# A two-layer kernel whose body is written as per-batch lists of single operations

## The chip, the cores and the metric

One core of one Trainium2 chip. The metric is the device time of one execution in microseconds (us); TensorE's granted clock is given where it bears on a reading. TensorE is called PE, VectorE DVE, ScalarE ACT, GpSimd POOL and SyncE SP, as in the profile.

## The reference

Attention with a threshold, then a gated layer that mixes over the sequence. Batch 8, 8 heads, 576 positions, head size 64; in and out are float32.

```python
scores = q @ k.T / 8                              # per batch and head: 576 x 576
scores = where(scores >= max(scores) - tau, scores, -1e9)
attn   = softmax(scores)
x      = concat_heads(attn @ v)                   # 8 x 576 x 512

h = relu(x @ w_in); u, v = h[..., :512], h[..., 512:]
v_s = w_spatial @ normalize(v) + b_spatial        # mixes positions
out = (u * v_s) @ w_out
```

## The kernel before

The work is cut into 144 steps, 18 for each batch. A step makes the scores of 128 queries of two heads in a three-bank PSUM tile, of which there are two. TensorE writes the main part (512 keys) in four 64x64 quadrants and the tail (the last 64 keys of both heads) with one 128x128 product. VectorE takes the maximum, ScalarE the exponential in two halves, then the mask makes p: on VectorE as one instruction, or, for some steps, on ScalarE (a steep Prelu in place of the first exponential, an exponential after it, and a small shift of the maximum on VectorE). p is transposed by a DMA and multiplied with v ("pv"). The gated layer's jobs (v, u, s, o) of earlier batches are spread over the steps.

```python
def on_act(i, c):                       # which masks ScalarE makes
    return c in (2, 4) or c == 0 and 0 < i < 6

def scores(i, c):
    s = ps_s.tile([P, 1536], F32, name="s")       # pool of two
    ...                                           # 4 main products, 64x64 quadrants
    for n, m, rows in tails:                      # the tail, straight behind them
        nc.tensor.matmul(out=view(s[rows], 512, ...), lhsT=qks[n][:, 0, m],
                         rhs=kd_ring[n % 2], start=True, stop=True)

def step(i, c, fs):                     # fs: this step's other jobs (multiply, evict)
    s = scores(i, c)
    while held: held.pop(0)()           # evictions left by the step before
    for kind, mm, ev in fs[:2]:
        mm()
        if kind == "act": ev()
    nc.vector.tensor_reduce(out=nm, in_=s, ..., op=ALU.max, negate=True)
    ...                                 # shift, VectorE evictions, exponentials
    if unmasked: mask()                 # mask and transpose of the step before
    for f in ready: f()                 # loads, stores, transposes of x
    for kind, mm, ev in fs[2:]:
        mm(); ...

# x: one transpose for each head pair (4 blocks of 128x128) and one per two pairs for their ends
nc.sync.dma_start_transpose(out=xts[b][:, hp, 0:512]..., in_=xn...)
nc.sync.dma_start_transpose(out=xts[b][:, hp, 512:640], in_=xn)

# ahead of the body: q, k, v of the first pairs, then
for j in range(3):
    load_w_in(j)
```

## Time and profile before

| | before |
|---|---|
| median of 4 runs (range) | 480.91 us (479.03 to 484.21) |
| span of the profiled run | 480.6 us, clock 0.992 |
| busy PE / DVE / ACT / POOL | 443.8 / 411.7 / 390.6 / 227.3 us |
| SP's time in issuing DMAs, summed from the trace | 381.5 us |

A batch is cut where its first maximum starts. The lines behind this are in the prediction.

### The profile page before, as it was taken

To read this page: it belongs to the slowest core of one execution; us is meant where nothing else is said; L and a number is where in the kernel's file an instruction comes from. 1 tells how busy PE (TensorE), PEld (TensorE's weight loads), DVE (VectorE), ACT (ScalarE), POOL (GpSimd) and SP (SyncE) were. 2 spreads that over 40 slices of the span, in tenths; PEclk is the share of its full clock that TensorE was granted. 3 is DMA by queue.
4 is the path that set the end of the run, shared out by engine and by line. 5 is a ranking of instruction groups with operands and counts; after the bars stand their busy time and mean duration, and the time that the engine had idled before them with its cause. 6 is when DMAs were issued, how large, how long until landed. Compare 5 with 4: busy or idle time off the path is not lost.

```text
span 480.6 us, 10876 instructions
## 1 busy us (share of the span) xinstructions
PE 443.8 (92%) x4153; PEld 225.9 (47%) x4203; DVE 411.7 (86%) x563; ACT 390.6 (81%) x677; POOL 227.3 (47%) x403
## 2 busy tenths in 40 slices
PE   7788888889999999999999999999997999999995
PEld 4344444444544445454544545444543545445542
DVE  4989898979989988999889997999887898898573
ACT  4799999989878897888889798888977689797251
POOL 3453344995347533674327553575416544253021
PEclk9899999999999999999999999999999999999999
DMA  7989899979999999988999899899999889667523
GB/s 231 247 179 210 191 222 195 206 158 210 196 164 189 195 199 205 236 151 176 221 211 183 160 210 224 178 192 200 194 192 168 180 164 217 136 114 119 149 86 112
DMA packets 226131, 88.55 MB, mean 184 GB/s; under 512 B 196896, under 2 KB 221600, under 8 KB 226080
## 3 DMA queue, kind: packets, MB, share of 16 engines
q1 hardware_dynamic: 225424, 86.98, 87.7%
q8 instruction: 33, 0.54, 0.5%
q0 software_dynamic: 160, 0.52, 0.3%
q10 hardware_dynamic: 496, 0.36, 0.2%
q14 instruction: 18, 0.15, 0.1%
HBM read 33.31 MB, written 9.44 MB: 89 GB/s over the span
## 4 chain that ended last, share of the span: by engine, by line
PE 45%; DVE 22%; ACT 22%; issue 7%; DMA 3%; POOL 0%; POOLq 0%; SPq 0%; ACTq 0%; DVEq 0%
PE s L576 14%; DVE negm L618 10%; DVE p L599 8%; ACT e L635 6%; PE s L580 6%; ACT e L641 5%; PE f L295 4%; PE f L478 4%; PE f L246 3%; ACT p L637 3%; PE f L537 2%; DMA pT<-p 2%; PE f L508 2%; ACT vrel L446 2%; PE f L290 2%
## 5 line engine op out<-in xcount | busy, mean ns | idle before, releaser
L618 DVE TENSOR_REDUCE negm<-s 128x2 f32<-128x1152 f32 x144 | 194.9, 1353 | 32.5 <-PE s L580 31.3
L576 PE MATMUL s<-qkT 64*64 64x512 f32 x1152 | 158.6, 621 | 14.5 <-ACT e L641 8.6
L599 DVE SCALAR_TENSOR_TENSOR p<-e,ctau 128x1152 bf16<-128x1152 f32 x91 | 133.7, 1469 | 1.2 <-ACT e L641 1.2
L641 ACT ACTIVATE e<-s,negm 128x576 f32<-128x576 f32 x182 | 124.9, 741 | 7.2 <-DVE negm L618 6.8
L580 PEld LDWEIGHTS s<-kd,qkT 128*128 128x128 f32 (+1 forms) x320 | 41.6, 178 | 118.4 <-issue 106.3
L635 ACT ACTIVATE e<-s,negm 128x576 f32<-128x576 f32 x106 | 72.9, 742 | 15.8 <-DVE negm L622 10.6
L269 POOL COPY kd<-qkT 64x64 f32<-64x64 f32 x62 | 28.0, 451 | 98.5 <-ACT qkT L264 96.7
L580 PE MATMUL s<-kd,qkT 128*128 128x128 f32 (+1 forms) x320 | 70.1, 323 | 0.0
L576 PEld LDWEIGHTS s<-qkT 64*64 64x64 f32 x1152 | 30.1, 132 | 46.6 <-ACT e L641 18.7
L454 POOL TENSOR_SCALAR nmean<-sm 128x1 f32<-128x1 f32 (+1 forms) x35 | 16.6, 474 | 71.1 <-ACT vrel L446 63.1
L295 PEld LDWEIGHTS <-pT 128*128 128x128 bf16 x1024 | 41.8, 97 | 9.1 <-issue 5.9
L295 PE MATMUL f<-v,pT 128*128 128x65 bf16 x992 | 44.9, 194 | 0.0
L637 ACT ACTIVATE p<-e 128x1152 bf16<-128x1152 f32 x37 | 43.0, 1163 | 1.2
L137 POOL COPY qn<-ql 128x640 f32<-128x640 f32 x31 | 32.6, 1052 | 16.2 <-DMA ql<-in_k_dram 11.6
L290 PE MATMUL f<-v,pT 128*128 128x130 bf16 x124 | 27.2, 219 | 7.0 <-DMA pT<-p 3.5
L508 PE MATMUL f<-wsT,vn 128*128 128x512 bf16 x119 | 31.1, 382 | 0.3
L466 POOL TENSOR_SCALAR vn<-vrel,rs,nm 128x512 bf16<-128x512 f32 (+1 forms) x34 | 28.5, 839 | 3.7
L478 PE MATMUL f<-xT,w_in 128*128 128x512 bf16 x97 | 27.6, 379 | 1.6 <-DVE xn L304 0.8
L436 PE MATMUL f<-w_in,xT 128*128 128x512 bf16 x102 | 28.2, 379 | 0.5
L253 ACT COPY qkT<-f 128x512 f32<-128x512 f32 x31 | 18.3, 590 | 12.8 <-PE f L246 12.2
L251 ACT ACTIVATE qkT<-f 128x512 f32<-128x512 f32 x31 | 18.3, 589 | 12.5 <-PE f L246 12.1
L304 DVE TENSOR_TENSOR xn<-f,r 128x256 bf16<-128x256 f32 x62 | 26.3, 425 | 2.1
(168 smaller groups left out, 647.9 us busy)
## 6 DMA issues: line engine op xcount, KB each, us to landing
vl<-in_v_dram SPq DMA_DIRECT2D x16, 512.0 KB, 4.5
ql<-in_q_dram SPq DMA_DIRECT2D x15, 512.0 KB, 4.9
kl<-in_k_dram SPq DMA_DIRECT2D x15, 512.0 KB, 4.4
out_dram<-oo SPq DMA_DIRECT2D x10, 512.0 KB, 3.6
uT<-in_moe_w_in_dram SPq DMA_DIRECT2D x3, 512.0 KB, 6.1
uT<-in_moe_w_spatial_dram SPq DMA_DIRECT2D x2, 576.0 KB, 5.6
vl<-in_v_dram SPq DMA_DIRECT2D x16, 64.0 KB, 4.3
pT<-p SPq DMA_TRANSPOSE x64, 5.0
```

Of the source, the lines that this page charges most:

```text
L137: nc.gpsimd.tensor_copy(out=t, in_=ld_ring[i // 2 % 2][w][:, 2 * (i % 2):2 * (i % 2) + 2].rearrange("p h c d -> p c h d"))
L290: nc.tensor.matmul(out=t[:, at:at + 130], lhsT=pt[:, 4, :], rhs=vt[:, 4:6, :].rearrange("p b d -> p (b d)"), start=True, stop=False)
L295: nc.tensor.matmul(out=t[:, at + 65 * h:at + 65 * h + 65], lhsT=pt[:, 5 * h + j, :], rhs=vt[:, 6 * h + j, :], start=False, stop=(h == 1 an ...
L478: nc.tensor.matmul(out=t, lhsT=w_in[:, m, f * P:(f + 1) * P], rhs=xts[b][:, m, 0:512], start=(m == 0), stop=(m == 3))
L508: nc.tensor.matmul(out=t, lhsT=vn[:, c, f * P:(f + 1) * P], rhs=wsT[:, c, 0:512], start=(c == 0), stop=(c == 4))
L576: nc.tensor.matmul(out=s[rows, 1024 * h:1024 * h + 512], lhsT=qks[n][halves[h], 0, m], rhs=qks[n][halves[h], 1, 0:512], start=True, stop=True)
L580: nc.tensor.matmul(out=view(s[rows], 512, [[448, 2], [1, 64]]), lhsT=qks[n][:, 0, m], rhs=kd_ring[n % 2], start=True, stop=True)
L599: nc.vector.scalar_tensor_tensor(out=pt[:, c % 2, :], in0=ef, scalar=ctau, in1=ef, op0=ALU.is_ge, op1=ALU.mult)
L618: nc.vector.tensor_reduce(out=nm, in_=s, axis=AX.X, op=ALU.max, negate=True)
L635: nc.scalar.activation(out=e[:, h, :], in_=s[:, h, :], func=ACT.Prelu, bias=nm[:, h:h + 1], scale=by, alpha=1e30)
L637: nc.scalar.activation(out=pr_ring[i // 2 % 2] if c == 4 else p_ring[2 * (i % 2) + c // 2][:, c % 2], in_=e.rearrange("p h s -> p (h s)"), ...
L641: nc.scalar.activation(out=e[:, h, :], in_=s[:, h, :], func=ACT.Exp, bias=nm[:, h:h + 1])
```

## The change

The intent is to let each engine have its own order. The body is no longer generated by `step`; it is a list of tokens for each batch. S is the main scores of a step, K their tail, M the maximum, B the shift, E and F the two exponentials, W a mask on VectorE, Z one on ScalarE, T a transpose of p, X one of x, L a load, Ci a load of w_in, and so on; ":1" means the batch before. There are four lists, the last serving batches 3 to 7. The order of the tokens is the order in which each engine gets its instructions.

```diff
+ORDER = [( ... ),            # 203, 240, 252 and 248 tokens
+ "S0:0 QA1:0 K0:0 qa1:0 v4:2 M0:0 S1:0 ev4:2 W17:1 QR1:0 K1:0 qr1:0 u1:2 E0:0 kd1:0 M1:0 F0:0 R1:1 "
+ ... )]
+ON_ACT = [(2, 4, 5, 9, 11, 13, 16), (0, 2, 4, 11, 13), (2, 4, 11, 13, 16), (2, 4, 7, 11, 13, 15)]
-    def scores(i, c): ...
-    def step(i, c, fs): ...
+    def main_scores(g): ...        # token S
+    def tail_scores(g): ...        # token K
+    def top(g): ...                # token M
+    ...
-                sends.append(lambda: nc.sync.dma_start_transpose(     # x, 4 blocks per head pair
-                    out=xts[b][:, hp, 512:640], in_=xn))              # and 1 for the ends
+    def send_x(m, n0, n1):                                            # two pairs and their ends
+        nc.sync.dma_start_transpose(out=to..., in_=xns[m][:, n0:n1, :]...)
-    ld_ring ... ("ql", 5), ("kl", 4), ("vl", 5)                       # ends loaded per two pairs
+    rest_ring, vx_ring                                                # ends loaded per batch
-        for j in range(3):
-            load_w_in(j)                                              # now tokens Ci2, Ci1, Ci0
+        for it in range(B):
+            for tok in ORDER[min(it, len(ORDER) - 1)].split():
+                run_token(tok, it)
```

## The prediction

> **What bounds the kernel now.** I read the page's engine table first, then busy time cut at every 18th maximum (a batch has 18 steps, each begun by one TENSOR_REDUCE on a score tile), then the costliest groups, the list of waits, and the timeline of one step and of the longest stall.
>
> The engine table: three engines are above 80%, so the average names no bound.
>
> ```profile
> PE 443.8 (92%) x4153; PEld 225.9 (47%) x4203; DVE 411.7 (86%) x563; ACT 390.6 (81%) x677; POOL 227.3 (47%) x403
> ```
>
> Busy time by stretch: the opening, batches 0, 1, 2, 4, 6, and the ending. Columns are the stretch, its length, busy us of each engine with the number of instructions, granted clock, DMA share, GB/s.
>
> ```profile
> 0.00:9.28 9.28, 6.62 (x35) 4.48 (x36) 3.62 (x26) 3.23 (x6) 3.27 (x14) 1.00 0.71 203
> 9.28:55.92 46.64, 38.79 (x367) 19.09 (x365) 41.52 (x51) 40.27 (x60) 21.57 (x39) 0.96 0.90 213
> 55.92:108.35 52.43, 44.42 (x459) 23.73 (x464) 46.33 (x60) 49.26 (x85) 32.14 (x54) 1.00 0.99 196
> 108.35:162.20 53.85, 51.20 (x506) 26.66 (x511) 49.05 (x63) 46.61 (x84) 30.20 (x52) 1.00 0.99 191
> ...
> 217.68:272.56 54.88, 53.60 (x507) 26.96 (x513) 49.65 (x63) 47.55 (x85) 28.18 (x49) 1.00 0.95 194
> ...
> 327.44:387.12 59.68, 55.21 (x507) 27.35 (x513) 49.75 (x63) 47.82 (x85) 27.86 (x49) 0.97 0.95 183
> ...
> 441.50:480.60 39.10, 33.86 (x260) 17.28 (x265) 21.55 (x51) 14.72 (x29) 5.55 (x7) 0.99 0.41 118
> ```
>
> Three regimes. Batch 0 has no second layer: PE is idle 7.9 us, DVE busy 89%, ACT 86%. Batch 1 is ScalarE's: 49.26 of 52.43 (94%). From batch 2 on PE is the bound: 53.60 of 54.88, 98%, with the DMA queues at 95 to 99% beside it. Batches 3, 5 and 7 took 55.48, 54.88 and 54.38. Batch 6 is the odd one, 4.8 us over its neighbours. The groups that I price with:
>
> ```profile
> L618 DVE TENSOR_REDUCE negm<-s 128x2 f32<-128x1152 f32 x144 | 194.9, 1353 | 32.5 <-PE s L580 31.3
> L599 DVE SCALAR_TENSOR_TENSOR p<-e,ctau 128x1152 bf16<-128x1152 f32 x91 | 133.7, 1469 | 1.2 <-ACT e L641 1.2
> L641 ACT ACTIVATE e<-s,negm 128x576 f32<-128x576 f32 x182 | 124.9, 741 | 7.2 <-DVE negm L618 6.8
> L637 ACT ACTIVATE p<-e 128x1152 bf16<-128x1152 f32 x37 | 43.0, 1163 | 1.2
> ```
>
> The timeline of one step in batch 4, then the stall of batch 6:
>
> ```profile
> 252.03 1.09 PE L576 MATMUL s<-qkT 64*64 64x512 f32 x8
> 253.05 0.49 PE L580 MATMUL s<-kd,qkT 128*128 128x128 f32 x2
> 253.38 1.03 PE L436 MATMUL f<-w_in,xT 128*128 128x512 bf16 x4
> ...
> 358.94 6.81 SPq L603 DMA_TRANSPOSE pT<-p  x1
> ...
> 369.36 0.23 PE L290 MATMUL f<-v,pT 128*128 128x130 bf16 x1 [3.19 <-DMA pT<-p]
> ...
> 371.49 1.99 PE L576 MATMUL s<-qkT 64*64 64x512 f32 x8
> ```
>
> Each PE job starts before the modelled end of the last one, so start to start counts: scores 1.02 us, their tail 0.33, four bf16 products 0.86. In batch 6 a transpose of p landed late, PE waited 3.19 us, and its next score set took 1.99 us instead of 1.09.
>
> **What the Trainium skill says.** "Perfetto Trace Analysis", Identifying the Most-Contended Engine, warns that matmul busy share is a poor measure of PE's headroom; here the starts support the 98%, since groups follow each other with no gap. "TensorE: Matmul & The Clock Gate", HAM oscillation, says an idle gap of some 3.4 us lets the clock fall; the trace agrees, with a gap of 3.19 us and a score set at half speed after it, mean clock 0.97. "SBUF — State Buffer", Who interferes with whom, says a VectorE instruction with two SBUF inputs and a GpSimd instruction that reads SBUF exclude each other; the mask is one of those, and a q copy that met it took 1.90 us against 0.72 us alone at 8.09. "DMA: Bandwidth & Descriptors", DMA Transpose (X-bar), says two transposing streams at once corrupt each other, so all of them stay on one queue; in the trace every transpose is issued by SP, and one of p holds that queue about 3.3 us.
>
> **The change part by part.**
> 1. The body. Each of the eight batches is now a written list of single operations, so maximum, shift, two halves of the exponential, mask, product and eviction each have their own place on their engine. Matmul work does not change: the instruction order has 5,261 PE rows against 5,260. No PE time is removed; only waits can be. The last two tokens and the remaining jobs leave the same nine gMLP jobs of batch 6 for after the body, so the ending is worth nothing: 39.1 stays. The opening loads and the first transposes are the same too: 9.3 stays.
> 2. Masks on ScalarE: batch 0 has 7 instead of 9, batch 1 5 instead of 8, batch 2 5 instead of 6, later 6 as before (one step moved). A mask leaving ScalarE saves it 1.16 us and costs VectorE 1.47 less the 0.25 us shift = 1.22. So batch 0: ACT 40.3 - 2.3 = 38.0, DVE 41.5 + 2.4 = 43.9. Batch 1: ACT 49.3 - 3.5 = 45.8, DVE 46.3 + 3.7 = 50.0. Batch 2: DVE 50.3, still under PE's 51.2. The bound of batch 1 changes engine and hardly falls.
> 3. SP queue. x is transposed for two head pairs and their ends in one piece: 38 transposes of x become 15, at 1.2 to 1.3 us of issue each, so about 28 us less. The 64-row ends of q, k, v are loaded per batch: 65 loads become about 34, at 0.62 us about 19 us less. 47 us over eight batches is 6 us of queue per batch, of about 44 used. Bytes fall only by the double load of v's ends, about 0.5 MB of 88.55, so the DMA engines stay as full as they are. This lies off the critical path except where a transpose of p comes late, as in batch 6.
> 4. w_in is loaded in the list instead of ahead of it: 2 MB no longer stand before the second group's q and k. At 13.9 to 19.6 us only POOL waited for these, so I give it nothing.
>
> Sum. A two-buffer cycle (scores 1.35, maximum 1.35, exponentials 1.37, some 0.8 for shift and handovers, an estimate) makes 4.9 us per two steps, 44 us for 18, and VectorE 43.9: batch 0 goes from 46.6 to 45.5. Batch 1: VectorE's 50.0 at 97%, 51.5. Batch 2: 53.2. Batch 3: 54.3. Batches 4 and 5: PE's 53.6 at 99%, 54.2 each. Batch 6: most of its 4.8 us goes with the lighter queue, 55.0. Batch 7: 53.6. With 9.3 and 39.1 that is 9.3 + 45.5 + 51.5 + 53.2 + 54.3 + 108.4 + 55.0 + 53.6 + 39.1 = 469.9, so 470 us, 2.1% less. Of the 10.7 us, 4.7 come from the stall of batch 6, 2.0 from batches 0 and 1, the rest from 0.7 to 1.2 us in each later batch.
>
> **The rivals.**
> Saturation: PE and DMA are both full, and the list only moves waits about. For it: PE's 98% and a DMA share of 0.95 to 0.99. Against it: 33 us of PE idle time in the whole run, a third of it in batches 0 and 1. Then 476 to 480.
> VectorE becomes the bound: it takes six more masks, 7.3 us, in batches where it had 88 to 91%; POOL's exclusions come on top. The list of waits puts 31.3 us of its idle time to score tails, so it can only fill that if scores come earlier. Then batches 0 to 2 keep their length: 473 to 477.
> Rigid order: each engine obeys one fixed order, with two PSUM banks for all jobs and two score tiles; a late operation holds what stands behind it, and a PE gap near 3 us also halves the clock. For it: the stall of batch 6 shows the price, some 5 us. A burst of a store, a merged x transpose and a 512 KB load ahead of a p transpose would repeat in each steady batch. Then 480 to 490.
> Better than expected: PE alternates now between scores and other jobs before the tail. Before, the tail follows the scores at 1.02 us in every step, so no row shows what another neighbour costs; 0.05 us per step would be 7 us either way. With that and no stall, 460 to 464.
>
> **Range and chances.** My sum is just at the 2% line (470.6). The better case and the sum's good side make 50% for faster; saturation and VectorE make 46%; the rigid order mostly ends within 2%, and 4% is left for slower. Range 461 to 480.
>
> **What would show it.** Right: steady batches of 54.0 to 54.5 us with PE at 99%; no PE wait of 3 us on a transpose of p and clock 1.00 in batch 6; batch 1 at 51 to 52 with DVE near 97% and ACT near 88%; SP idle longer; opening and ending within 0.5 us. Wrong: a steady batch under 53 (then PE's busy time held removable cost), or over 55; batch 0 or 1 shorter by over 3 us (then the cycle and not VectorE's work was the limit); new waits of PE for evictions by ScalarE; or an ending that moves by over 2 us.

## The result, and the profile after

| | before | after |
|---|---|---|
| median of 4 runs (range) | 480.91 us (479.03 to 484.21) | 463.68 us (462.81 to 464.75) |
| ratio | | 0.964 (95%: 0.958 to 0.969) |
| opening | 9.3 | 9.5 |
| batch 0, 1, 2 | 46.6, 52.4, 53.9 | 44.5, 51.1, 53.1 |
| batch 3, 4, 5 | 55.5, 54.9, 54.9 | 52.1, 53.4, 53.6 |
| batch 6 | 59.7 | 53.6 |
| batch 7 and ending | 93.5 | 91.3 |

Ratios are the mean time of one kernel's fast runs over that of the other's in the same rounds, so not quite the ratio of the medians. Rows below the ratio are from the two profiled runs.

The engine table of the changed kernel:

```profile
PE 430.0 (93%) x4147; PEld 224.2 (49%) x4203; DVE 417.7 (90%) x558; ACT 380.1 (82%) x673; POOL 209.2 (45%) x434
```

PE has 13.8 us less busy time, with the same matmuls; a few us of this are missing records, since runs of the changed list whose traces lack none have PE busy for 433.3 us (masks elsewhere) to 436.1 (w_in earlier), and the kernel before, profiled again, 443.8. The stretches show where: opening, batches 0, 1, 2, 4, 6, ending, with the columns explained in the prediction.

```profile
0.00:9.45 9.45, 7.46 (x37) 5.10 (x41) 3.72 (x22) 3.26 (x6) 2.06 (x9) 1.00 0.73 207
9.45:53.93 44.48, 37.19 (x368) 18.50 (x361) 42.57 (x50) 37.89 (x59) 16.34 (x34) 1.00 1.06 238
53.93:105.01 51.08, 45.43 (x462) 23.37 (x467) 49.12 (x58) 45.61 (x81) 31.44 (x58) 1.00 0.96 194
105.01:158.12 53.11, 50.70 (x505) 26.64 (x512) 51.47 (x64) 45.17 (x83) 32.51 (x63) 1.00 0.94 190
...
210.18:263.55 53.37, 50.95 (x504) 26.74 (x510) 50.28 (x64) 46.56 (x84) 24.29 (x53) 1.00 0.99 200
...
317.13:370.74 53.61, 51.29 (x506) 26.91 (x512) 50.43 (x64) 46.77 (x85) 24.78 (x53) 1.00 0.98 203
...
420.69:462.01 41.32, 35.87 (x300) 18.63 (x301) 23.35 (x53) 16.32 (x32) 7.42 (x13) 0.99 0.40 114
```

In batch 4 PE is busy 50.95 us where it was 53.60, with 504 matmul records against 507. Both lack some, the changed kernel more. Here are batches 4 and 5 together in two traces that lack none (4203 of 4203): the kernel before, profiled again, and the changed list with w_in loaded earlier (its order differs in batch 0 alone):

```profile
218.16:327.90 109.74, 107.97 (x1027) 53.95 (x1025) 100.04 (x127) 95.05 (x169) 57.15 (x98) 1.00 0.98 196
```

```profile
216.32:322.59 106.27, 103.81 (x1026) 53.56 (x1024) 99.92 (x128) 93.67 (x169) 47.74 (x108) 1.00 1.01 204
```

So PE's work falls from 54.0 to 51.9 us per batch, 2.1 us. Batch 0 shrank although DVE has a little more to do; it is now busy 96% of the batch. A part of its 2.1 us is not the change's: the kernel before ran its batch 0 at a mean clock of 0.96 in the first profile, and in the second at 1.00, where it took 46.0 us. The timeline says where PE's time went. Here is a stretch of batch 5 of the changed kernel, with the weight loads (PEld) that belong to the matmuls:

```profile
267.39 1.09 PE L651 MATMUL s<-qkT 64*64 64x512 f32 x8
268.41 0.55 PEld L614 LDWEIGHTS <-gT 128*128 128x128 bf16 x4 [0.81 <-issue]
268.42 1.04 PE L614 MATMUL f<-w_o,gT 128*128 128x512 bf16 x4
269.07 0.41 PEld L661 LDWEIGHTS s<-kd,qkT 128*128 128x128 f32 x2
269.29 0.38 PE L661 MATMUL s<-kd,qkT 128*128 128x128 f32 x2
269.51 0.60 PE L308 MATMUL f<-identf,kn 128*128 128x128 f32 x4
```

The tail (L661) no longer stands behind its scores (L651): a product of the gated layer does. The tail's weight load starts at 269.07, under that product, 0.22 us ahead of its matmul, and the tail takes 0.22 us start to start. Before, load and matmul of the tail began together at 253.05, as the scores ended, and it took 0.33. The product that now follows the scores starts 1.03 us after them, as the tail did, so it pays no more for the place than the tail did. Over all tails between 105 and 420 us, worked out from the trace, the median is 0.224 us between two other jobs (70 tails), 0.358 from a tail to scores behind it (19), and 0.325 still directly behind scores (18). In the kernel before all are in the last class.

The tails are not the whole of it. Worked out from the two full traces above as starts less idle time, per batch, the tails fall from 6.0 to 5.05 us, the scores from 18.3 to 18.0, and all other jobs from 29.6 to 28.9. For the scores a reason shows: in the changed list 16 of 107 score sets stand directly behind another, and the next starts 0.91 us after them, not 1.02. How the other jobs' 0.7 us comes about is not shown. The same place of the kernel before, with its weight load:

```profile
253.05 0.30 PEld L580 LDWEIGHTS s<-kd,qkT 128*128 128x128 f32 x2 [0.81 <-issue]
```

In the Trainium skill, "TensorEngine Tiling (Array Packing)", Key Properties, states "Changing tiling mode (not just tile) drains the TensorE". The scores use 64x64 tiles and the tail 128x128, and the trace agrees as far as it goes: whatever of another shape stands behind the scores, tail or product, starts, with its weight load, about 1.02 us after them (median), a further score set after 0.91. The changed kernel has fewer such changes, but only by those 16 pairs of 107 sets. What differs in most steps is what stands exposed behind one: a float32 tail and its load, or a bf16 product.

The waits of PE over the whole run, first of the kernel before and then of the changed one (in total, times, longest):

```profile
PE s L576 <- ACT e L641: 8.6, 16, 1.1
PE s L576 <- ACT e L635: 4.1, 6, 1.3
...
PE f L290 <- DMA pT<-p: 3.5, 2, 3.2
```

```profile
PE s L661 <- ACT e L683: 6.3, 9, 1.4
PE s L651 <- ACT e L683: 4.8, 7, 1.5
PE f L355 <- DMA pT<-p: 3.1, 6, 0.7
```

PE waits no less than before for exponentials; the wait of 3.2 us on a transpose is gone. And the groups that the masks concern:

```profile
L669 DVE TENSOR_REDUCE negm<-s 128x2 f32<-128x1152 f32 x144 | 194.6, 1352 | 8.9 <-PE s L661 4.8
...
L698 DVE SCALAR_TENSOR_TENSOR p<-e,ctau 128x1152 bf16<-128x1152 f32 x97 | 141.3, 1458 | 1.2 <-ACT e L686 0.4
```

Six masks more on DVE, and its idle time ahead of the maximum fell from 32.5 to 8.9 us.

### The profile page after: what moved, and what is told of

It is laid out like the page before. It is cut to its first block, busy times and chain, and to the rows that moved or that the text cites. A ratio compares the mean times of both kernels' runs of the same rounds, so it can differ in the third digit from the quotient of the medians.

```text
span 462.0 us, 10935 instructions
## 1 busy us (share of the span) xinstructions
PE 430.0 (93%) x4147; PEld 224.2 (49%) x4203; DVE 417.7 (90%) x558; ACT 380.1 (82%) x673; POOL 209.2 (45%) x434
## 4 chain that ended last, share of the span: by engine, by line
PE 37%; DVE 30%; ACT 16%; DMA 9%; issue 5%; SPq 1%; POOL 0%; POOLq 0%; ACTq 0%; DVEq 0%
DVE negm L669 15%; PE s L651 11%; DVE p L698 10%; DMA pT<-p 7%; ACT e L683 5%; ACT e L686 4%; PE s L661 3%; PE f L360 3%; PE f L614 3%; PE f L308 2%; ACT pr L703 2%; DVE xn L369 2%; PE f L585 2%; PE f L555 2%; ACT vrel L516 1%
## 5 line engine op out<-in xcount | busy, mean ns | idle before, releaser
L651 PE MATMUL s<-qkT 64*64 64x512 f32 x1152 | 153.5, 612 | 6.8 <-ACT e L683 4.8
L686 ACT ACTIVATE e<-s,negm 128x576 f32<-128x576 f32 x194 | 136.6, 746 | 15.5 <-DVE negm L669 12.3
L698 DVE SCALAR_TENSOR_TENSOR p<-e,ctau 128x1152 bf16<-128x1152 f32 x97 | 141.3, 1458 | 1.2 <-ACT e L686 0.4
L683 ACT ACTIVATE e<-s,negm 128x576 f32<-128x576 f32 x94 | 65.1, 737 | 21.5 <-DVE negm L675 20.3
L661 PE MATMUL s<-kd,qkT 128*128 128x128 f32 (+1 forms) x320 | 62.6, 297 | 8.4 <-ACT e L683 6.3
L661 PEld LDWEIGHTS s<-kd,qkT 128*128 128x128 f32 (+1 forms) x320 | 45.0, 182 | 48.8 <-issue 28.2
L651 PEld LDWEIGHTS s<-qkT 64*64 64x64 f32 x1152 | 31.0, 131 | 36.7 <-ACT e L683 12.2
L360 PEld LDWEIGHTS <-pT 128*128 128x128 bf16 x1024 | 41.9, 98 | 1.8 <-issue 0.5
L332 POOL COPY kd<-qkT 64x64 f32<-64x64 f32 x62 | 15.7, 253 | 57.9 <-ACT qkT L326 56.0
L369 DVE TENSOR_TENSOR xn<-f,r 128x256 bf16<-128x256 f32 (+1 forms) x94 | 35.5, 378 | 2.9
L703 ACT ACTIVATE p<-e 128x1152 bf16<-128x1152 f32 x31 | 36.4, 1173 | 0.2
L355 PEld LDWEIGHTS <-pT 128*128 128x128 bf16 x128 | 12.5, 98 | 32.7 <-issue 23.0
L188 POOL COPY kn<-kl 128x512 f32<-128x512 f32 x31 | 24.3, 783 | 6.3 <-DMA kl<-in_k_dram 3.5
L538 POOL TENSOR_TENSOR rs<-rs,mhalf 128x1 f32<-128x1 f32 (+1 forms) x35 | 25.0, 715 | 2.9
```

Of the source, the lines that this page charges most:

```text
L355: nc.tensor.matmul(out=t[:, at:at + 130], lhsT=pt[:, 4, :], rhs=vt[:, 4:6, :].rearrange("p b d -> p (b d)"), start=True, stop=False)
L360: nc.tensor.matmul(out=t[:, at + 65 * h:at + 65 * h + 65], lhsT=pt[:, 5 * h + j, :], rhs=vt[:, 6 * h + j, :], start=False, stop=(h == 1 an ...
L369: nc.vector.tensor_tensor(out=dst, in0=o[ps, g0:g1, 0:64], in1=r[ps, g0:g1].unsqueeze(2).broadcast_to([ps.stop - ps.start, g1 - g0, 64]), ...
L651: nc.tensor.matmul(out=s[halves[k], 1024 * h:1024 * h + 512], lhsT=qks[n][halves[h], 0, m], rhs=qks[n][halves[h], 1, 0:512], start=True, s ...
L661: nc.tensor.matmul(out=view(s[rows], 512, [[448, 2], [1, 64]]), lhsT=qks[n][:, 0, m], rhs=kd_ring[n % 2], start=True, stop=True)
L683: nc.scalar.activation(out=e, in_=s, func=ACT.Prelu, bias=bias_, scale=scale if steps[g][1] == 4 else 1.0, alpha=1e30)
```

## The experiments

Theory 1: most of the gain is PE's own time, because the tail left its place behind the scores. Theory 2: it is waits, taken out by the orders. Then come the parts one by one. Each experiment was timed beside the kernel before on its chip, whose medians were 478.7 to 480.8 us.

### The tail put back behind the scores

```diff
+        if kind == "K":
+            return
-            {"S": main_scores, "K": tail_scores,
+            {"S": lambda g: (main_scores(g), tail_scores(g)),
```

> The changed kernel with one thing put back: every tail of a score tile follows its main scores directly on TensorE, as before the change. Theory 1 (neighbours on TensorE): between 105 and 420 us of the changed kernel a tail between two other jobs takes 0.224 us start to start, directly behind the scores 0.325 us, so about 0.1 us in about 16 of 18 steps is paid again: PE busy rises from 430 to 440 to 444 us, steady batches from 53.6 to 55 us, the time from 463.7 to 470 to 475 us. Theory 2 (waits): the gain came from each engine's own order alone; then PE busy stays at 430 to 433 and the time within 2 us of 463.7.

473.82 us, ratio to before 0.985 (0.979 to 0.991): 10 us of the gain given back. Its batch 5, a steady one:

```profile
268.59:323.57 54.98, 53.57 (x514) 26.64 (x512) 50.43 (x64) 46.84 (x85) 23.86 (x53) 1.00 0.91 193
```

PE is back at 53.57 us and the batch at 54.98, against 53.60 and 54.88 in batch 5 before the change. In batches 4 and 5 the place of the tail makes the whole difference. The edit also parts the pairs of score sets, as a tail now stands between them: tails, scores and other jobs are back at 6.2, 18.35 and 29.1 us per batch. Theory 1 holds there; the 6 or 7 us that stay gained lie elsewhere.

### The tail split off in the kernel before, two ways

First, in each step, one job between scores and tail:

```diff
         ...                              # main products of scores()
+        between()                        # evictions held, then fs[0]'s multiply
         for n, m, rows in tails:
```

> The kernel before with one thing of the change done alone: in every step that has another job for TensorE, the first of them stands between the main scores and their tail. Theory 1: PE busy falls from 443.8 by 8 to 12 us, steady batches from 54.9 to 53.3 to 53.8 us, the time from 480.5 to 470 to 475 us. Theory 2: the time stays within 2 us of before, or gets longer because the maximum starts up to 1 us later in each step.

502.95 us, ratio 1.047 (1.042 to 1.053): 22 us slower, a miss for theory 1; theory 2 had named the way, a later maximum, but not the size. The tails did get shorter, mean record 283 ns against 323, yet PE busy did not fall by the 8 to 12 us expected: it is 443.5 us. By the same working as above, in batches 4 and 5 the tails lost 1.0 us per batch, while scores gained 0.3 and other jobs 0.4. And the maximum, which needs the tail, now starts a job later in each step:

```profile
L623 DVE TENSOR_REDUCE negm<-s 128x2 f32<-128x1152 f32 x144 | 194.9, 1354 | 54.6 <-PE s L586 53.7
```

DVE's idle time ahead of the maximum rose from 32.5 to 54.6 us. So I tried the split that delays no tail: the next step's scores trade places with this step's last job.

```diff
         for kind, mm, ev in fs[2:]:      # and likewise in fs[:2]
+            if then and mm is fs[-1][1]:
+                scores(*then)            # main part of the next step, one job early
             mm()
```

> The kernel before, with the split done so that no tail is delayed: the main scores of the next step change places with the last job of a step, so that this job stands between them and their tail, which comes where it came. Theory 1 (a tail between two other jobs costs 0.1 us less): PE busy falls from 443 to 432 to 435 us and the time to 470 to 476 us. Theory 2 (the split is only worth it in the new order, as the first split in the kernel before cost 22 us): the scores now wait for the exponentials of two steps earlier, PE's waits for ScalarE grow by what the tail saves, and the time is within 4 us of before or above it.

562.62 us, ratio 1.173 (1.165 to 1.180): 83 us slower. Theory 2's wait came, but theory 2 had it grow only by what the tails save. PE's waits of that run:

```profile
PE s L577 <- ACT e L651: 62.8, 58, 2.3
PE s L577 <- ACT e L645: 25.4, 19, 2.0
```

88 us of waiting where there were 13. The scores of a step need the tile that two steps earlier was read by ScalarE. In steps 54 to 125 of the kernel before, by the trace, a tile is held 5.06 us on average from the start of its scores to the end of its second exponential, and the next scores in it start 1.19 us later: 6.25, two periods of 3.12. The last job stood in that 1.19 us; scores moved ahead of it wait, and the job waits behind them. In the changed kernel a tile is held 5.33 us and the slack is 0.58, two periods of 2.95. The list takes half the slack out. My reading is that theories 1 and 2 are not rivals: the saving is PE's time, and the new order for the other engines lets it be taken. Shown is less: with the new list the place of the tail is worth 10 us, and two ways of splitting it off in the old frame both lose. A third way there was not tried.

### The masks where they were

The tokens were changed for the old places: B behind M, and Z where W stood, or the reverse.

```diff
-ON_ACT = [(2, 4, 5, 9, 11, 13, 16), (0, 2, 4, 11, 13), (2, 4, 11, 13, 16), (2, 4, 7, 11, 13, 15)]
+ON_ACT = [(2, 4, 5, 7, 9, 11, 13, 14, 16), (0, 2, 4, 5, 7, 11, 13, 16), (2, 4, 7, 11, 13, 16), (2, 4, 7, 11, 13, 16)]
```

> The changed kernel with the masks on ScalarE where the kernel before had them (9, 8, 6, 6 of 18 instead of 7, 5, 5, 6, and step 16 instead of 15). If the placing of masks brought a part of the gain, batches 0 to 2 (44.5, 51.1, 53.1 us) get longer by 2 us or more in sum and the time is 465.5 to 468. By the prediction the bound of batch 1 only changes engine, and the time stays within 1.5 us of 463.7.

472.33 us, ratio 0.983 (0.978 to 0.988): 8.6 us given back, far more than I expected. Batches 0 to 2 are 2.1, 0.9 and 1.0 us longer; the later ones, where only steps 15 and 16 trade roles, 0.3 to 0.9 each, batch 7 by 1.8. In batch 0:

```profile
8.79:55.42 46.63, 37.55 (x369) 18.66 (x361) 40.52 (x50) 39.81 (x61) 16.57 (x35) 1.00 1.09 235
```

DVE and ACT are both at 85 to 87%, so no engine's load explains it. A new wait of PE points at the places:

```profile
PE f L296 <- DVE xn L310: 5.4, 5, 1.7
```

A pv product waits for a bank that DVE empties late. The new tokens stand where I put them, and a list fitted to these masks could do better, so this shows what the fit is worth, not what the placing is worth by itself.

### w_in ahead of the body, and the reverse in the kernel before

```diff
+        for f in range(3):
+            load_w_in(f)
+            done.add((f"Ci{f}", 0))
         for _ in range(14):              # first transposes, before the lists run
```

> The changed kernel with three of the four loads of w_in issued ahead of the body, as before. By the prediction this is worth nothing: within 1 us of 463.7. A rival, that 1.5 MB ahead of the second group's q and k delays the first batch, expects batch 0 longer by 1.5 to 3 us.

469.92 us, ratio 0.977 (0.972 to 0.982): 6.2 us given back, all in batch 0, which takes 51.3 us and not 44.5. Waits in batch 0 of that run:

```profile
PEld f L308 <- POOL qn L188: 5.1, 1, 5.1
POOL qn L188 <- DMA ql<-in_q_dram: 4.3, 1, 4.3
PE f L308 <- POOL qn L188: 4.2, 1, 4.2
```

The list asks for the transposes of pair 2 at step 3; with 1.5 MB ahead of it q is late, POOL waits, PE waits 4.2 us, and the mean clock of the batch falls to 0.93. The same move in the kernel before:

```diff
-        for j in range(3):
-            load_w_in(j)
+    for j, g in enumerate((3, 6, 8)):
+        chores[g] = (load_w_in, j)       # shaped at steps 10, 11, 12
```

> The kernel before, with the three early loads of w_in issued at steps 3, 6 and 8 of the body and not ahead of it. If loading it ahead delayed the kernel before as it delayed the changed kernel (+6 us there), batch 0 falls from 46.6 to about 42 to 44 us and the time by 3 to 5 us. If only the new list, which asks for the second group's q earlier, feels it, the time stays within 1.5 us of before.

483.28 us, ratio 1.009 (1.002 to 1.015): no gain, rather a small loss. Batch 0 took 49.1 us, with a wait of 2.0 us for a transpose of p. At these steps, at least, a late w_in is no gain by itself; the new list needs it.

### The transposes of x

```diff
-        to = xt_of(m // 2)[:, m % 2, n0 * P:n1 * P]
-        nc.sync.dma_start_transpose(...)
+        for lo, hi in ((0, 4), (4, 8), (8, 9)):
+            if lo >= n0: nc.sync.dma_start_transpose(...)    # same bytes, three pieces
```

> The changed kernel with each merged transpose of x issued in its three pieces (4, 4 and 1 blocks) at the same place of the list: same bytes, some 23 more transposes on the SP queue at 1.2 to 1.3 us of issue each, 28 us in all. If the shorter queue brought a part of the gain, steady batches grow by 1 us or more and the time is 467 to 475. If the queue has slack enough, the time stays within 1.5 us of 463.7.

Fast runs 475.9 to 480.0 us, ratio to before 0.995 (0.988 to 1.002): some 12 to 15 us given back. The profiled execution took 825 us and counts for nothing here (see the end). So it was run again for a profile, with a variant that issues each piece soon after it is ready, behind the next transpose of p.

> The kernel of e7 again, unchanged, for a profile in the fast state (the one taken had TensorE at half speed throughout). Theory A expects 475 to 480 us, the issue of transposes of x at about 50 us in sum against 23, and waits of PE, or of VectorE through PE, for transposes of p or x that grow by some us per batch, with PE busy unchanged near 430.

> The changed kernel with x transposed in pieces again (38 transposes instead of 15), but each piece issued behind the first transpose of p after it is ready, as in the kernel before, and not three together at one place. Three together cost 12 us over the changed kernel. Theory A (SP's queue: 28 us more of issue push later transposes of p back, whose landing PE already waits for): spreading them helps little, 470 to 478 us. Theory B (only the burst of three at one place hurts): 463 to 467 us.

Again 477.36 us for the first, and 472.74 us, ratio 0.984 (0.977 to 0.992), for the spread pieces. The wait of PE for transposes of p, three together, then spread:

```profile
PE f L355 <- DMA pT<-p: 14.6, 13, 3.3
```

```profile
PE f L355 <- DMA pT<-p: 7.6, 9, 2.0
```

It was 3.1 in the changed kernel. The transposes of x hold SP 51.6 and 47.9 us in these two runs, 23.1 in the changed kernel, 50.0 in the kernel before: in the kernel before, a piece of 4 blocks takes a median of 1.26 us of issue and one of 1 block 1.23, in the changed kernel one of 9 blocks 1.56. With more of the queue's time in transposes of x, those of p land later, and the product with v has no time to spare for them: PE's wait for them grew by 11.5 us for three together. The loss is uneven, 7.2 us of it in batch 3 and 2.7 in batch 0, where the mean clock fell to 0.95 and 0.96 besides. Theory A fits: spreading recovers a part, not all.

### The kernel before again

> The kernel before, unchanged, profiled once more: whether batch 6 is again 4.8 us longer than its neighbours behind a late transpose of p. If it is a fixed collision in its queue, it comes again at the same place and 59 to 60 us; if it is chance, batch 6 takes 54.5 to 55.5 us and the profiled time is 476 to 478 us.

480.27 us. Batch 6 took 57.2 us, so it is again the longest, by 2.3 us over batch 5 and not 4.8. In it:

```profile
PE f L290 <- DMA pT<-p: 2.3, 1, 2.3
```

The collision comes back in the same batch, with a size that varies. The changed kernel's profile has no wait there over 0.7 us.

### What bounds the changed kernel

A probe: the maximum over 512 keys. Its output is wrong, which doesn't matter for the time.

```diff
-  in_=view(s_ring[g % 2], 0, [[960, 2], [1, S]])
+  in_=view(s_ring[g % 2], 0, [[960, 2], [1, 512]])
```

> A probe of what bounds the changed kernel now, wrong in its result on purpose: the maximum is taken over 512 of 576 keys, so VectorE's TENSOR_REDUCE falls from 1.35 to about 1.2 us, 2.4 us per batch. If VectorE (93 to 97% busy) bounds the batches, they shrink by 1.5 to 2.4 us each, 12 to 18 us in all; if TensorE (96%) or the DMA queues (0.98) bound them, by under 0.7 us each, under 5 us in all, most of it in batches 0 to 2.

461.32 us, ratio to before 0.961 (0.956 to 0.966), which overlaps that of the changed kernel. DVE lost 14.6 us of busy time (417.7 to 403.1) and the time some 1 by the ratios, 2.4 by the medians. DVE does not bound the steady batches, though it is busy 94%. The chain that ended last passes through all of them; two of its longest pieces in batch 5 of the changed kernel are landings:

```profile
284.19 6.27 DMA xT<-xn
...
307.86 6.51 DMA pT<-p
```

No run here removes PE's or the DMA's share alone, so which of the two sets the remaining 53.5 us is left open.

An attempt at a better version: the body's stores from POOL's queue.

```diff
-            nc.sync.dma_start(out=rows[...], in_=pair_o[b, c // 2])
+            nc.gpsimd.dma_start(out=rows[...], in_=pair_o[b, c // 2])     # and the ends' store
```

> An attempt at a version better than both: the changed kernel with the stores of the body (some 17) issued by GpSimd, so that SP's queue loses 0.55 us of issue for each and no transpose stands behind a store. Theory A expects 0.5 to 1.5 us per batch less, 455 to 461 us; if the chain through the queue is set by the transposes' own time to land, the time stays within 1.5 us of 463.7; if issuing from GpSimd costs its engine 1 us at a bad place, it gets longer by up to 3 us.

468.30 us, ratio 0.977 (0.971 to 0.983): slower than the changed kernel by 4.6 us. In its profile batches 4 and 5 are 0.4 us shorter, but batch 0 takes 1.2 us more, and batch 6 takes 57.2 us, with a wait of PE of 3.1 us for a transpose of p. POOL's issues took 0.56 to 0.78 us each. The changed kernel stays the best version.

## Why the prediction was right or wrong

The time, 463.7 us, lies in the range, and the direction was a coin toss that fell right. The sum of 470 was short by 6 us; the predicted saving was 10.7 and the span lost 18.6.

- "No PE time is removed; only waits can be": wrong, and the main failure. Some 2.1 us of PE time per steady batch is gone, 1.0 of it in the tails, which take 0.10 us less each between other jobs, and putting the tail back cost 10 us. The fourth rival named this very place, said that no row could tell, and sized it at 0.05 us per step, where 2.1 us per batch is 0.12; the time fell in its 460 to 464 us. The tiling page of the Trainium skill that I had not drawn on says that a change of tiling drains PE; with it I could have asked what stands exposed behind the scores.
- Steady batches at 54.2: they came at 53.4 and 53.6, and batch 3 at 52.1 for 54.3. Its "wrong if" for a batch under 53 fired for batch 3. The idle time of PE, which I let shrink to 1%, did not shrink (1.6% before, 2.3% in the changed list, by the two full traces): the saving lay under the busy time, not in the gaps.
- Batch 6: 53.6 for 55.0; the stall is gone, as forecast. But its 4.8 us was counted as a fixed cost, and a second profile of the kernel before shows 2.3. That the lighter queue removed it is not shown: with x in pieces again batch 6 took 54.55 us, and with the stores off the queue 57.2.
- SP's queue: the amount was right (42 us less issue, 47 predicted). "Off the critical path except where a transpose of p comes late, as in batch 6" was wrong: in the new list it costs 9 to 15 us when put back, most of it in batches 0, 1 and 3.
- Masks: the bound of batch 1 did move to DVE as worked out, 51.1 us for 51.5, with DVE at 96%. Batch 0 came at 44.5 for 45.5, better than the sum of the two-buffer cycle, with DVE at 96%. But in the list these places are worth 8.6 us, not the 2 us I gave batches 0 and 1.
- w_in "nothing": right for the old frame (it loses a little), wrong for the new list, 6.2 us. Ahead of the body stood three loads, 1.5 MB, not 2.
- Opening: right (+0.2 us). Ending: predicted unchanged; cut at the end of the last maximum in both kernels, it is 1.6 us longer, while batch 7 before it is 3.8 us shorter. The prediction's 39.1 was cut 0.6 us later, and against it the ending grew by 2.2, past its sign of 2. Together batch 7 and ending are 2.2 us less.
- "Rigid order" did not come in this kernel, but several edits of its list paid as that rival describes: waits on banks, on q, on a transpose.

The parts put back cost 10, 8.6, 6.2 and 12 to 15 us, about 38 us for a gain of 17. They cannot be added: each was undone in a list fitted to all the others. The merged loads of the ends were not put back by any run, so what they are worth is not shown.

Two readings in the prediction were off without changing its sum: PE's idle time before is 36.8 us (480.6 less 443.8) and not 33, with 15.9 of it in batches 0 and 1; and "98% from batch 2 on" is 95% in batch 2. The 5,261 and 5,260 PE rows are of an instruction order that no run here shows; the traces have 4203 weight loads each.

## What to carry to other kernels

Before calling a busy engine's time fixed, look at which neighbours its instructions have: if one order is all that the trace shows, the cost of another is unknown, and an experiment on one pair of neighbours settles it. A saving on a saturated engine may need the other engines' orders to free its buffers in time; tried alone it can lose many times its worth. Before reading a small difference of busy time, count the records. And undoing one part of a tuned order measures the fit of the order as much as the part.

## What the Trainium skill lacked or had wrong

- "TensorEngine Tiling (Array Packing)", Key Properties, has the drain at a change of tiling but no size: here a float32 128x128 product directly behind 64x64 ones takes 0.325 us start to start, between other 128-row jobs 0.224. A set of 64x64 products is followed after 1.02 us by either a tail or a bf16 product, after 0.91 by another such set.
- "DMA: Bandwidth & Descriptors", DMA Transpose (X-bar), gives no time that a transpose holds the issuing queue (the page has cycles for older generations elsewhere, for other sizes): here medians of 1.23 us for 1 block of 128x128, 1.26 for 4, 1.56 for 9, and 3.3 to 3.5 for 18.
- "TensorE: Matmul & The Clock Gate", HAM oscillation, speaks of gaps over some 3.4 us, and the section behind it of short, frequent idling without a length: here the score set fell to 1.99 us after a wait of 3.19, and one in batch 0 of the kernel before took 1.98 us after waits of 1.29 and 1.13 us one step apart. Both times the trace grants half the clock for 3.41 us.
- "TensorE: Matmul & The Clock Gate" tells of a clock stuck low for 50 us and more, no page of this: one execution of the kernel with x in pieces ran at about half speed throughout, 825 us against 476 to 480, with PE busy 801 us and its score matmuls at a mean of 1125 ns for about 612. Its trace has no record of the clock. It did not come again in four more runs of the same program.
